# One more set of seven products: the first layer of expert 0 for the last 512 tokens, mixed with second-layer outputs

## The chip, the cores and the metric

The kernel runs on one core of a Trainium2 chip. The metric is device time in microseconds (us). Engine names are those of the profile: PE is the matrix engine, PEld its weight loads, DVE the vector engine, ACT the scalar engine, POOL the GpSimd engine, SP the engine that issues most transfers.

## The reference

Two stages. The first is an attention with positive features: for each of 8 batches and 8 heads, `phi(x) = [exp(p), exp(-p)]` with `p = x @ w_phi` less its largest absolute value; then `phi(q) @ (phi(k)^T v)` divided by `phi(q) . sum(phi(k))`. Its result is the token matrix `x` of 4608 rows and 512 columns. The second is a mixture of 8 experts without selection:

```python
P = np.exp(logits)                      # 4608 x 8, logits = x @ w_gate
for _ in range(8):
    P /= P.sum(1, keepdims=True) + 1e-09
    P /= P.sum(0, keepdims=True) + 1e-09
    P *= N / E
for e in range(E):
    h = np.maximum(x @ w1[e], 0.0)      # 512 -> 1024
    ye = h @ w2[e]                      # 1024 -> 512
    out += P[:, e:e + 1] * ye
```

Every expert works on every token; the eight rounds of row and column scaling are called the routing below.

## The kernel before, in words

**Tokens.** The 4608 tokens lie transposed in the tile `xT`, in nine groups of 512. Groups 0 to 7 hold the first 512 rows of each batch, group 8 the 64 remaining rows of all eight. An accumulator tile `acc[g]` holds the output of a group.

**Expert 0** is computed plainly. `up0(g, part)` (L798) makes two slices of 128 hidden columns of group g: for each, four matmuls of 512 columns into a PSUM bank, then a ReLU on ACT into a tile of the ring `hT` (L776). A group has eight slices. `down0(g, part)` (L802) makes 128 tokens of output: eight matmuls of 512 columns, then a copy into `acc` (L811 on ACT; L818 on DVE for the even parts of groups 0 to 4). Names used below: u60 is part 0 of `up0` for group 6, d53 is part 3 of `down0` for group 5.

**Experts 1 to 7** use seven products instead of eight block products in both layers. `sums_w` (L1014) forms sums and differences of weight quadrants on DVE, some into tiles of the ring `T` (eight tiles). The sums of `x` quadrants are made once: `pair_sums_x(p)` (L1078) for the pairs of groups (0,1), (2,3), (4,5), (6,7), four DVE operations of 1024 columns each into tiles of the ring `S` (five tiles), and `sums_x(8)` (L1094) for group 8, four of 512 columns. All are written to DRAM (`xd`) by SP and read back by `load_x` before each use. `up7` (L1134) makes the first layer. Per block of hidden columns it has the products x1, x2, x3, x4 (which add up in one PSUM bank, an ACT copy L1189 into the ring `U` being taken after each of the first three, and an ACT ReLU L1198 after the last), w1 and w2 in a second bank, y1 in a third. Three DVE operations (L1193) add a bank and a copy, apply the ReLU and write `hT`. For a pair of groups a product is two matmuls of 512 columns (L1163); for group 8 alone four of 256 columns (L1129). `down7` (L1241) makes the second layer, with DVE sums of hidden values into `S` and seven products X1 to Z2. The string `ORDER` (L1407) interleaves a group's `up7` products with the `down7` products of an earlier group, which a list named `queue` holds.

**What sets the order of the work.** Nothing above issues at once. Each call records an operation in a planner (class `Plan`, L112): an engine, an assumed duration, the keys that it reads and writes, and the tiles that it needs. `schedule` then takes, again and again, the operation that can start first by the planner's own clock; among equal starts it takes the one recorded first. A tile ring or a PSUM bank that is not free delays a start. The resulting order on each engine is fixed in the program. On the chip each engine works through its list in order and waits on semaphores.

**Around the change.** The attention stage ends with a planner operation `swap` (L910) that releases the attention's tiles and writes the key "late"; four more `hT` tiles, the rings `T`, `S`, `U`, and the accumulators of groups 5 to 8 exist only from then on. After it come, in the written order: the routing (L937 to 970, eight rounds on DVE, lines L952 to L966, each with one small fp32 matmul of `cs` with `colw` on PE; the result is `P`); the rest of expert 0, `fill` (L908), which alternates the parts of `up0` for groups 6, 7, 8 with the parts of `down0` for groups 5, 6, 7; and then expert 1, with `load_w`, the sums of x, `sums_w` and `up7`. `sums_w` of expert 1 reads `P`, so its DVE operations come after the routing. The first product x1 of expert 1 reads two of those sums and all four tiles that `load_x` brought for the first pair. The list `queue` starts with an empty entry for the first half of expert 1's first pair and the four parts of `down0(8)` for its second half.

Of the kernel before, what the change touches and what calls it, by code (L numbers as in the profile page):

```python
# [12 lines left out]
ALU = mybir.AluOpType  # L13
# [215 lines left out]
def kernel(  # L229
# [535 lines left out]
    def up(w1, g, hT, fcs, n, r=(), w=()):  # L765

        for f0 in fcs[::n]:
            ph = new(f"P{n}")
            ht = hT[f0 // 2]
            for i in range(n):  # L770
# [8 lines left out]
                [ph], [(ht, f0 + i) for i in range(n)])  # L779

    def down(w2, hT, tss, r=()):
        py = new(f"P{len(tss)}")
        for i, ts in enumerate(tss):
            for fc in range(8):
# [4 lines left out]
                    [(hT[f // 2], f) for f in (range(8) if fc == 0 else (fc,))]  # L789
# [13 lines left out]
    def down0(g, part):  # L803
        tss = (part,)
        py = down(W[0][1], hts[g], tss, akey(g))
# [3 lines left out]
        for i, ts in enumerate(tss):  # L809
            if ts % 2 or g >= NA:  # L810
# [126 lines left out]
    def routing():  # L937
        c_bc = None
        for it in range(8):
# [6 lines left out]
            else:  # L946
# [3 lines left out]
                def u(ub=ub):  # L950
# [63 lines left out]
    def sums_w(e, w1, w2):  # L1014

        eng = pool if e == 0 else dve
# [49 lines left out]

    def xq(g, i, j):

        return lambda: xT[:, 2 * i:2 * i + 2, 512 * g + 256 * j:512 * g + 256 * j + 256]
# [8 lines left out]
    def pair_sums_x(p):  # L1078
# [7 lines left out]
        for n, y, z, r in ((0, b12, b11, ["sums of x"]), (1, b22, x(0), [X[0]]),  # L1086
                           (2, b22, b12, []), (3, b21, x(1), [X[1]])):
            sub(dve, 1024, x(n), y, z, ALU.subtract,
# [5 lines left out]
    def sums_x(g):  # L1094

        X = [new("S") for _ in range(2)]

        def x(n):
            return lambda: X[n // 2]()[:, n % 2 * 2:n % 2 * 2 + 2]

        b11, b12, b21, b22 = xq(g, 0, 1), xq(g, 0, 0), xq(g, 1, 1), xq(g, 1, 0)
        for n, y, z, r in ((0, b12, b11, []), (1, b22, x(0), [0]), (2, b22, b12, []),
                           (3, b21, x(1), [1])):
            sub(dve, 512, x(n), y, z, ALU.subtract,
                xkeys(g) + ["late", "sums of x"] + [(X[i // 2], i % 2) for i in r]
                + ([(X[1], "slot")] if n == 2 else []),
                [(X[n // 2], n % 2)] + ([(X[1], "slot")] if n == 0 else []))
        for i in range(2):
            dma("SP", 1 << 18, 250, lambda i=i: nc.sync.dma_start(
                out=Xd[4][i], in_=X[i]().rearrange("p (k a) b -> p k (a b)", k=2)),  # L1110
                [(X[i], n) for n in range(2)], [("Xd", 4, i)])

# [21 lines left out]
    def up7(A, p, X, H, r0):  # L1134
# [3 lines left out]
        gs = (2 * p, 2 * p + 1) if pair else (8,)  # L1138
        xk = [k for g in gs for k in xkeys(g)]

        def b(n):
            i, j = {"11": (0, 1), "21": (1, 1), "22": (1, 0)}.get(n, (0, 0))
            if n[0] != "t":
                if pair:
                    return lambda k: xT[:, 2 * i + k, 1024 * p + 512 * j:][:, 0:512], []
                return lambda k: xT[:, 2 * i + k, 4096 + 256 * j:][:, 0:256], []
            t = int(n[1]) - 1
            if pair:
                return lambda k: X[t]()[:, k, :], [X[t]]
            return lambda k: X[t // 2]()[:, t % 2, 256 * k:256 * k + 256], [X[t // 2]]  # L1150
# [53 lines left out]
        more += [k for n in ("s2", "s3", "22") for k in A[n][1]] + X + list(r0)  # L1204
# [280 lines left out]
```

## Time and profile before

| | us |
|---|---|
| median of three runs | 1029.73 |
| lowest, highest | 1029.61, 1030.56 |
| the profiled execution, device time | 1032.67 |
| its span in the profile | 1030.9 |
| PE busy in the span | 1013.7 |
| DVE, ACT, POOL busy in the span | 861.9, 710.7, 465.0 |

The profiled execution took 2.94 us more than the median; its span leaves out 1.8 us of it. Times of day in the text ("at 246 us") count from the start of the span. A PE row gives the first start, the time from there to the modelled end of the last matmul, the line, and the number of matmuls; as matmuls overlap, the distance between the starts of two rows is the better measure of what the first one took. Idle time ahead of a row, and what ended it, stands in brackets where it is long enough to be shown.

### The profile page before, as it was taken

The page shows a single profiled execution, that of the slowest core. Times are in us where ns is not written, and L with a number is a line of the kernel's source. Part 1 is how long each engine was busy: PE and PEld are TensorE (multiplying, and loading weights), DVE is VectorE, ACT ScalarE, POOL GpSimd, SP SyncE. Part 2 cuts the span into 40 slices and gives each one's busy share as a digit, 9 for nine tenths or more (in the row PEclk, how much of TensorE's full clock was granted, in tenths as well). Part 3 has the DMA queues.
Part 4 walks back from the last instruction along what each step waited for, and adds up shares of the span by engine and source line. Part 5 has one row for each costly group of instructions (what it writes and reads, how often), then busy time and mean ns, then how long its engine had stood idle before and what let it go on. Part 6 is the DMA issues. An engine that isn't in the chain of part 4 may idle for free.

```text
span 1030.9 us, 21864 instructions
## 1 busy us (share of the span) xinstructions
PE 1013.7 (98%) x7958; PEld 690.5 (67%) x7958; DVE 861.9 (84%) x1852; ACT 710.7 (69%) x1577; POOL 465.0 (45%) x534
## 2 busy tenths in 40 slices
PE   7899999999999999999999999999999999999998
PEld 5656666644566766676667766676667666776665
DVE  7999998987777878888888888898878888888776
ACT  7999999846588866665666666665665666665663
POOL 5876765400244354344434454435443544443443
PEclk9999999999999999999999999999999999999999
DMA  9999996085411233121611161116112341103333
GB/s 243 179 172 143 175 167 96 23 212 156 83 42 42 63 85 81 42 63 41 123 42 42 31 124 48 57 32 118 47 43 62 68 98 42 57 27 83 139 126 125
DMA packets 124316, 93.77 MB, mean 91 GB/s; under 512 B 47456, under 2 KB 115872, under 8 KB 124208
## 3 DMA queue, kind: packets, MB, share of 16 engines
q1 hardware_dynamic: 90448, 68.44, 24.9%
q0 software_dynamic: 33680, 23.90, 16.3%
q8 instruction: 62, 1.02, 0.4%
q14 instruction: 46, 0.38, 0.1%
q10 hardware_dynamic: 80, 0.03, 0.0%
HBM read 94.98 MB, written 14.16 MB: 106 GB/s over the span
## 4 chain that ended last, share of the span: by engine, by line
PE 91%; DVE 4%; DMA 3%; SPq 1%; issue 0%; ACT 0%; POOL 0%; DVEq 0%
PE P L1129 40%; PE P L1163 32%; PE P L484 17%; PE P L683 1%; DMA qkT<-qk 1%; DMA acc<-in_q_dram 1%; DVE acc L1302 1%; DVE m L476 1%; DVE w L1012 1%; DMA v_r<-in_v_dram 1%; PE P L722 1%; DVE hT L1193 0%; SPq L406 0%; DVE xb L703 0%; PE P L688 0%
## 5 line engine op out<-in xcount | busy, mean ns | idle before, releaser
L1316 POOL TENSOR_TENSOR acc<-acc,V 128x512 f32<-128x512 f32 x244 | 313.7, 1297 | 421.4 <-ACT V L1312 418.1
L1189 ACT COPY U<-P 128x512 f32<-128x512 f32 x378 | 215.5, 588 | 133.1 <-PE P L1163 105.2
L1312 ACT ACTIVATE V<-P 128x256 f32<-128x256 f32 x488 | 212.4, 475 | 121.3 <-PE P L1129 117.8
L1193 DVE CUSTOM_DVE_ANT_0 hT<-P,U 128x512 bf16<-128x512 f32 x378 | 252.1, 687 | 42.9 <-ACT U L1189 22.9
L1129 PEld LDWEIGHTS <-S 128*128 128x128 bf16 x1984 | 194.1, 98 | 52.6
L1302 DVE SCALAR_TENSOR_TENSOR acc<-P,acc 128x256 f32<-128x256 f32 x372 | 159.8, 477 | 68.4 <-PE P L1129 65.7
L1163 PE MATMUL P<-xT,w 128*128 128x512 bf16 x728 | 200.7, 379 | 1.1 <-DVE acc L1302 1.1
L1129 PEld LDWEIGHTS <-hT 128*128 128x128 bf16 x1488 | 145.6, 98 | 54.8
L1163 PE MATMUL P<-xT,T 128*128 128x512 bf16 x560 | 160.6, 379 | 0.0
L1129 PE MATMUL P<-w,hT 128*128 128x256 bf16 x992 | 143.1, 273 | 0.0
L1129 PE MATMUL P<-T,S 128*128 128x256 bf16 x1056 | 136.8, 273 | 0.0
L1163 PEld LDWEIGHTS <-w 128*128 128x128 bf16 x896 | 87.6, 98 | 61.7 <-issue 0.8
L1129 PE MATMUL P<-w,S 128*128 128x256 bf16 x928 | 123.5, 273 | 0.0
L1012 DVE TENSOR_TENSOR S<-hT 128x512 bf16<-128x512 bf16 x248 | 105.6, 440 | 21.0 <-PE P L1129 20.0
L1163 PEld LDWEIGHTS <-T 128*128 128x128 bf16 x672 | 65.7, 98 | 58.4 <-issue 2.1
L476 DVE TENSOR_REDUCE m<-P 128x4 f32<-128x512 f32 x128 | 83.5, 677 | 3.9 <-PE P L484 3.0
L609 POOL TENSOR_TENSOR v<-v_m,em 128x512 bf16<-128x512 f32 x64 | 66.9, 1045 | 42.7 <-ACT em L480 39.9
L1198 ACT ACTIVATE hT<-P 128x512 bf16<-128x512 f32 x126 | 74.2, 597 | 12.1 <-PE P L1163 11.9
L484 PE MATMUL P<-w,hT 128*128 128x512 bf16 (+1 forms) x328 | 81.7, 374 | 0.2 <-DVE m L476 0.2
L484 PE MATMUL P<-xT,w 128*128 128x512 bf16 x288 | 74.6, 379 | 0.3 <-ACT q L480 0.3
L480 ACT ACTIVATE k<-P 128x512 bf16<-128x512 f32 x128 | 68.5, 628 | 4.3 <-PE P L484 3.0
L480 ACT ACTIVATE q<-P 128x512 bf16<-128x512 f32 x128 | 69.3, 636 | 1.1 <-PE P L484 0.7
(109 smaller groups left out, 1177.2 us busy)
## 6 DMA issues: line engine op xcount, KB each, us to landing
xT<-xd SPq DMA_DIRECT2D x168, 128.0 KB, 2.2
w<-in_moe_w_dram POOLq DMA_DIRECT2D x14, 1024.0 KB, 9.9
v_m<-in_v_dram SPq DMA_DIRECT2D x14, 512.0 KB, 5.1
out_dram<-acc SPq DMA_DIRECT2D x12, 512.0 KB, 3.1
X<-xd SPq DMA_DIRECT2D x42, 128.0 KB, 2.2
early<-xd SPq DMA_DIRECT2D x42, 128.0 KB, 2.2
xd<-S SPq DMA_DIRECT2D x18, 256.0 KB, 3.3
qk<-in_k_dram POOLq DMA_DIRECT2D x12, 256.0 KB, 6.0
```

The lines of the kernel that those rows point to most:

```text
L476: dve(el, lambda: nc.vector.tensor_reduce(out=dst(), in_=src(), axis=AX.X, op=ALU.max, apply_absolute_value=True), r, w)
L480: act(el, lambda: nc.scalar.activation(out=dst(), in_=src(), func=ACT.Exp, bias=0.0, scale=scale), r, w)
L484: nc.tensor.matmul(out_, lhsT=lhsT, rhs=rhs, start=start, stop=stop)
L1012: lambda: f.tensor_tensor(out=out_(), in0=x(), in1=y(), op=op), r, w, **kw)
L1129: pe(256, lambda i=i, k=k, z=z: nc.tensor.matmul(bank()[:, 256 * i:256 * i + 256], lhsT=lhs(k, i), rhs=rhs(k), start=first and z, stop=k = ...
L1163: pe(512, lambda k=k: nc.tensor.matmul(bank[fp](), lhsT=f()[:, k, 128 * fp:128 * fp + 128], rhs=rhs(k), start=first and k == 0, stop=k == ...
L1189: act(512, lambda: nc.scalar.copy(out=u[fp][n]().rearrange("p a b -> p (a b)"), in_=x[fp]()), [x[fp]], [u[fp][n]])
L1193: dve(500, lambda: nc.vector._custom_dve(ADD_SAT, out=out_(fp, i, j), in0=halves_(bank[fp]()), in1=flat(u[fp][n]()), s0=3.0e38, s1=0.0), [ ...
L1198: act(512, lambda: nc.scalar.activation(out=out_(fp, i, j), in_=halves_(x[fp]()), func=ACT.Relu, bias=0.0, scale=1.0), [x[fp]], [okey(fp, ...
L1302: dve(330, lambda n=n, ts=ts: nc.vector.scalar_tensor_tensor(out=acc[g][:, ts, 256 * j:256 * j + 256], in0=bank()[:, 256 * n:256 * n + 256 ...
L1312: act(390, lambda n=n: nc.scalar.activation(out=u()[:, n, :], in_=bank()[:, 256 * n:256 * n + 256], func=ACT.Copy, bias=0.0, scale=P[:, 4 ...
L1316: pool(670, lambda: nc.gpsimd.tensor_tensor(out=acc[g][:, 2 * i:2 * i + 2, 256 * j:256 * j + 256], in0=acc[g][:, 2 * i:2 * i + 2, 256 * j: ...
```

## The change

- `sums_w1_first()` is new: four DVE operations of 1024 columns that form the sums of expert 0's first weight matrix, into four tiles of `T`. The quadrants themselves stay as they are, since `up0` reads them too.
- `sums_x` now takes its two tiles from `T` instead of `S`, and hands them on. For group 8 they are still written to DRAM.
- The calls of `sums_x(8)` and of the four `pair_sums_x` move in the written order from expert 1, behind `fill`, to the place right behind `routing()` and ahead of the rest of expert 0. (The short description says "ahead of the routing"; the call of `routing()` stands first in the diff.)
- Group 8's first layer of expert 0 goes through `up7` with those sums: per block of 256 hidden columns 28 matmuls of 256 columns, three copies and one ReLU (two slices at once) on ACT and three additions on DVE. There are two such blocks.
- `fill` is replaced by a written list, `FILL`: u60 to d62. Behind it the products of group 8 are interleaved by `ORDER` with d63, d70, d71, d72. The list `queue` now holds d73 for the first half of expert 1's first pair; the four parts of `down0(8)` stay in its second half.
- Keys of `hT` tiles are adapted (`hkeys`, `down`, `up`).

```diff
-    def down(w2, hT, tss, r=()):
+                [ph], [(ht, (f0 + i) % 2) for i in range(n)])
+    def hkeys(g, f):
+        return range(2) if g == 8 else (f % 2,)
+
+    def down(g, w2, hT, tss, r=()):
...
-    def expert0(i):
-        if i < 4 * NG:
-            up0(i // 4, i % 4)
-        down0(i // 4 - 1, i % 4)
-
-    fill = range(4 * NA + 4, 4 * NG)
...
-    routing()
-    grant("X", 4, {id(d): d for key in [("L", g) for g in range(NG)] + ["colw"]
-                   for d in plan.readers[key]}.values())
-    for i in fill:
-        expert0(i)
...
+    def sums_w1_first():
+
+        w1 = W[0][0]
+        S = [new("T") for _ in range(4)]
+        wk = [(w1, n) for n in range(4)]
+
+        def q(i, j):
+            return lambda: w1()[:, 2 * j:2 * j + 2, 512 * i:512 * i + 512]
+
+        def s(n):
+            return lambda: S[n]().rearrange("p (a b) -> p a b", a=2)
+
+        for n, y, z, op, r in ((0, q(0, 0), q(0, 1), ALU.add, []),
+                               (2, q(1, 0), q(0, 0), ALU.subtract, []),
+                               (1, s(0), q(1, 0), ALU.subtract, [S[0]]),
+                               (3, q(1, 1), s(1), ALU.subtract, [S[1]])):
+            sub(dve, 1024, s(n), y, z, op, wk + ["late"] + r, [S[n]])
+        return {"11": (q(1, 0), wk), "12": (q(1, 1), wk), "22": (q(0, 1), wk),
+                "s1": (s(0), [S[0]]), "s2": (s(1), [S[1]]), "s3": (s(2), [S[2]]),
+                "s4": (s(3), [S[3]])}
...
     def sums_x(g):
 
-        X = [new("S") for _ in range(2)]
+        X = [new("T") for _ in range(2)]
...
-    def up7(A, p, X, H, r0):
+    def up7(A, p, X, H, r0, g=8):
...
-    queue = [(0, 8, {}, None, None), (0, 8, {"X1": 0, "X2": 1, "Z1": 2, "Y1": 3}, None, None)]
+    FILL = (
+        "u60 u61 u62 u63 d50 u70 d51 u71 d52 u72 d53 u73 d60 d61 d62").split()
+    MIX = ("63", "70", "71", "72")
+    queue = []
...
+    CHUNK = ("X1", "X2", "Z1", "Y1")
+    routing()
+    grant("X", 4, {id(d): d for key in [("L", g) for g in range(NG)] + ["colw"]
+                   for d in plan.readers[key]}.values())
+    A0 = sums_w1_first()
+    X0 = {8: sums_x(8)}
+    for p in range(4):
+        pair_sums_x(p, dve)
+    for i in FILL:
+        (up0 if i[0] == "u" else down0)(int(i[1]), int(i[2]))
+    for g in (8,):
+        H = [[new("hT") for _ in range(2)] for _ in range(2)]
+        hts[g] = H[0] + H[1]
+        un = up7(A0, 5, X0[g], [H], ["late"], g)
+        mix = iter(MIX)
+        for n in ORDER:
+            if len(n) == 3:
+                un[n[:2], int(n[2])]()
+            elif n in CHUNK:
+                i = next(mix, None)
+                if i:
+                    down0(int(i[0]), int(i[1]))
+    queue += [(0, 7, {"Y1": 3}, None, None),
+              (0, 8, {"X1": 0, "X2": 1, "Z1": 2, "Y1": 3}, None, None)]
+
     for e in range(1, E):
...
         if e == 1:
-            for p in range(4):
-                pair_sums_x(p)
-            sums_x(8)
```

More of the change, by code (lines that the diff above doesn't have):

```diff
@@ L1014, in sums_w @@
     def sums_w(e, w1, w2):
-        eng = pool if e == 0 else dve
+        eng = dve
         def q(w, i, j):
@@ L1203, in up7 @@
         more = [("banks", 0), ("banks", 1)]
-        more += [k for n in ("s2", "s3", "22") for k in A[n][1]] + X + list(r0)
+        more += [k for n in ("s2", "s3", "22") for k in A[n][1]] + list(r0)
+        more += [k for _, key in X for k in key]
         def x1(fp):
```

36 lines of the change are left out of this document (21 added, 15 removed).

## The prediction

> **What bounds the kernel now.** I read the head of the page first, then the table of stretches, the waits of PE, and the timelines of PE and DVE from 200 to 285 us, where the change lies.
>
> ```profile
> PE 1013.7 (98%) x7958; PEld 690.5 (67%) x7958; DVE 861.9 (84%) x1852; ACT 710.7 (69%) x1577; POOL 465.0 (45%) x534
> ```
>
> PE is busy for 98% of the span; the rest has to lie in few places. The table of stretches (PE, PEld, DVE, ACT and POOL busy, granted clock, DMA share, GB/s) finds them:
>
> ```profile
> 200.00:250.00 50.00, 49.99 (x343) 25.76 (x342) 41.72 (x98) 27.29 (x52) 2.65 (x5) 1.00 0.63 169
> 250.00:300.00 50.00, 49.55 (x293) 28.43 (x291) 37.49 (x72) 37.32 (x74) 11.40 (x10) 1.00 0.42 85
> ...
> 1000.00:1031.00 31.00, 26.86 (x196) 18.84 (x193) 18.96 (x38) 11.31 (x26) 12.24 (x10) 0.97 0.36 136
> ```
>
> From 200 to 250 us PE has no idle time, from 250 to 300 us 0.45 us, and the last stretch holds the tail. All that PE waited for between 200 and 1000 us is one row:
>
> ```profile
> PE P L1163 <- DVE acc L1302: 1.1, 5, 0.5
> ```
>
> So in the stage of the change, and in all that follows, time is PE work, end to end. A change there gains what it takes off PE and loses each hole that it makes. The granted clock is 1.00 throughout; nothing here moves it.
>
> The profiled execution took 1032.67 us, 2.94 more than the median of 1029.73. My sum is made as a difference against the profiled execution (its span of 1030.9 plus 1.8 around it) and then put on the median.
>
> **PE work.** Removed: 8 slices x 4 matmuls of 512 columns. Their price is the distance between rows of eight:
>
> ```profile
> 246.83 1.89 PE L484 MATMUL P<-xT,w 128*128 128x512 bf16 x8
> 248.56 1.89 PE L484 MATMUL P<-w,hT 128*128 128x512 bf16 x8
> 250.28 0.59 PE L1163 MATMUL P<-xT,w 128*128 128x512 bf16 x2
> ```
>
> 1.73 us for eight, 216 ns each: 32 x 216 = 6.90 us. Added: 7 products x 2 blocks x 4 matmuls = 56 of 256 columns. The same stage, group 8 through seven products mixed with second-layer products, exists for the later experts; the chain has it as one unbroken piece:
>
> ```profile
> 560.70 12.24 PE P L1129 x112
> ```
>
> 12.24/112 = 109.3 ns: 56 x 109.3 = 6.12 us. PE saves 0.78 us. The chunks of the second layer (d63 to d83) are the same in number and move only in order.
>
> [...]
>
> **ACT and DVE work.** Unit prices:
>
> ```profile
> L1193 DVE CUSTOM_DVE_ANT_0 hT<-P,U 128x512 bf16<-128x512 f32 x378 | 252.1, 687 | 42.9 <-ACT U L1189 22.9 <-PE P L1163 11.0 <-PE P L1129 3.0
> L1189 ACT COPY U<-P 128x512 f32<-128x512 f32 x378 | 215.5, 588 | 133.1 <-PE P L1163 105.2 <-PE P L1129 22.1 <-DVE S L1012 0.3
> ...
> L776 ACT ACTIVATE hT<-P 128x512 bf16<-128x512 f32 x72 | 43.1, 635 | 8.9 <-PE P L484 8.8
> ...
> L1012 DVE TENSOR_TENSOR T<-w 128x1024 bf16<-128x1024 bf16 x28 | 20.2, 722 | 0.1
> ```
>
> These are the DVE addition, the ACT copy, the ACT ReLU of 512 columns and the DVE sum of weights. ACT loses 8 ReLUs (5.1 us) and gets 6 copies and 2 ReLUs (4.8 us): nothing to speak of. Its stage has room:
>
> ```profile
> 209.10:246.30 37.20, 37.19 (x194) 17.64 (x191) 30.19 (x68) 18.03 (x32) 1.47 (x2) 1.00 0.83 223
> ```
>
> ACT is busy for 18.0 of these 37.2 us, which is the cover. DVE is another matter: it gets 4 sums of weights x 0.69 (as T<-w) and 6 additions x 0.69, 6.9 us, in a stage in which it is busy for 30.2 of 37.2 us, 7.0 idle. Nearly all of that idle time is inside the routing, while a round waits for PE's small matmul:
>
> ```profile
> L966 DVE RECIPROCAL c_bc<-P 128x8 f32<-128x8 f32 x8 | 1.7, 208 | 6.1 <-PE P L484 5.4 <-ACT acc L811 0.7
> ```
>
> **What moves without cost.** The sums of x are 20 operations before and after. Their new written place can hardly start them earlier: the first five ran at once, and the sixth waited for a tile of `S` to come free.
>
> ```profile
> 212.23 0.63 DVE L1012 TENSOR_TENSOR S<-xT 128x1024 bf16<-128x1024 bf16 x1
> ...
> 224.82 0.64 DVE L1012 TENSOR_TENSOR S<-xT,S 128x1024 bf16<-128x1024 bf16 x1
> ```
>
> The four sums of group 8 do come earlier, since they now take `T`; they leave the stretch behind 235 us and enter the one at 210 us, a zero sum on DVE. Their two writes to DRAM move ahead of eleven others in SP's list; each waits for its two sums. Who needs them is group 8 of expert 1, some 50 us later, and the tiles read back for the first pair are due only when expert 1 begins: 0. `T` has eight tiles: four for the weight sums, two for x, two left for the routing, which holds about one at a time. The sums of expert 1 find two at once and the others when group 8's products end, before they are due: 0, with the risk kept for the range. PSUM: six banks for the two blocks, one for an output chunk, one for the routing's matmul, eight of eight. A late bank would delay a round by about one ACT copy, 0.6 us; I take 0, because the six are not all held at once. POOL's two weight transfers of expert 1 start at "late" as before; the second matrix of expert 2 can be fetched somewhat earlier, since d80 to d83 end earlier; nobody waits for it: 0.
>
> **When expert 1 can begin.** This decides the sign. Rows at the end of the routing (`P`, then sums of expert 1):
>
> ```profile
> 245.96 0.46 DVE L968 TENSOR_TENSOR P<-T,c_bc 128x288 f32<-128x288 f32 x1
> 246.34 0.68 DVE L1012 TENSOR_TENSOR T<-w 128x1024 bf16<-128x1024 bf16 x1
> 247.06 0.69 DVE L1012 TENSOR_TENSOR w<-w 128x1024 bf16<-128x1024 bf16 x1
> 247.78 0.69 DVE L1012 TENSOR_TENSOR T<-w 128x1024 bf16<-128x1024 bf16 x1
> ```
>
> The second T<-w ends at 248.5 us; with it x1 has its operands, and it started at 250.28, 1.8 us later, when PE was done with `fill`. So today the routing has 1.8 us of slack.
>
> The 6.9 us of new DVE work lie ahead of `P`: the weight sums have to precede group 8's products, and these come on PE before the routing ends. Bounds of the delay: 0.8 us if all of 6.1 us of idle time in the L966 row is used, 6.9 us if none is. I take 4.5, nearer the upper end, because a round that has group 8's sums of x ahead of its answer still waited:
>
> ```profile
> 237.92 0.21 DVE L966 RECIPROCAL c_bc<-P 128x8 f32<-128x8 f32 x1 [1.19 <-PE P L484]
> ```
>
> Those 1.19 us passed with DVE empty: the sums at hand had run out or came between the steps, where they delay the chain. x1's operands are then ready at 253.0 us (249.3 to 255.4).
>
> What PE can do without them: all of `fill` (till 250.28), less 0.78, plus d80 to d83, which before lay inside expert 1's first pair:
>
> ```profile
> L484 PE MATMUL P<-w,hT 128*128 128x512 bf16 x32 | 8.5, 379 | 0.0
> ```
>
> 32 x 0.216 = 6.9 us, so till 256.4 us, 3.4 us after the operands. PE need not stop. But those chunks had a use:
>
> ```profile
> L484 PE MATMUL P<-w,hT 128*128 128x512 bf16 x8 | 2.4, 379 | 0.0
> ```
>
> ```profile
> L484 PE MATMUL P<-w,hT 128*128 128x512 bf16 x8 | 2.2, 379 | 0.0
> ```
>
> These rows group PE's timeline from 253.7 to 258.2 and from 265.9 to 269.1 us. The first eight chunk matmuls stand in the first half of the pair, where the written order puts none: the planner pulled them in where a product waited for a copy or an addition. The other eight stand among the second half's last products, by the written order or for the same reason. Without filler the pair would lose between 8 x 0.216 = 1.7 and 16 x 0.216 = 3.5 us. With 3.4 us of it left, it loses between 0 and 0.1. To this I add the sums of expert 1: five of them (S3 and four of w2, 3.5 us at the rows' price) now run when x1 has begun, and delay its additions; before, the 1.8 us of slack let two or three of these run ahead of x1. I take 0.5 us of holes in all, ends 0 and 3.5.
>
> **What PE loses in the routing today.** Rows around three of the small matmuls (two passes each):
>
> ```profile
> 214.28 0.28 PE L484 MATMUL P<-cs,early 128*128 128x8 f32 x2
> 214.42 1.46 PE L484 MATMUL P<-xT,w 128*128 128x512 bf16 x6
> ...
> 217.61 0.36 PE L484 MATMUL P<-cs,early 128*128 128x8 f32 x2
> 217.82 1.89 PE L484 MATMUL P<-xT,w 128*128 128x512 bf16 x8
> 219.55 1.46 PE L484 MATMUL P<-w,hT 128*128 128x512 bf16 x6
> 220.95 0.36 PE L484 MATMUL P<-cs,early 128*128 128x8 f32 x2
> ```
>
> The first takes 0.14 us of PE's time, with no wait. Between the other two lie 14 matmuls, 3.02 us; the distance is 3.34. In sum:
>
> ```profile
> L484 PE MATMUL P<-w,hT 128*128 128x512 bf16 x96 | 23.4, 379 | 0.0
> L484 PE MATMUL P<-xT,w 128*128 128x512 bf16 x85 | 20.3, 379 | 0.0
> L484 PE MATMUL P<-cs,early 128*128 128x8 f32 x16 | 2.6, 233 | 0.0
> ```
>
> 181 x 0.216 + 8 x 0.14 = 40.2 of the 41.0 us from 209.3 to 250.28: 0.8 us are lost by waiting. With more DVE work between the steps the planner may place these matmuls better or worse: between -0.8 and +0.8, I take 0, the middle, as the rows show both a matmul without a wait and two with one.
>
> **Sum.** -0.78 + 0.5 = -0.3 us: the profiled execution would take 1032.4, the median 1029.4 us. This is within 0.2% (2.06 us), which is about what a measurement of this kernel can tell from no change.
>
> **Rivals.**
>
> 1. Slower: expert 1 waits for the routing. DVE at 81% gets 6.9 us more in the one serial chain of the stage. If x1's operands come late, chunks d80 to d83 are used up ahead of x1, the first pair loses up to 3.5 us, and beyond 256.4 us PE stands still one for one. The loss reaches 2.06 us above before when the holes reach 2.84 us, with operands at 255.7 us: 2.7 us later than I think and just past the upper bound of the DVE sum. For it: the planner puts x1 at the moment at which it believes the sums ready, so the old slack of 1.8 us is gone, and the planner believes rounds shorter than they are (3.02 against 3.34 us). Against: 7.0 us of idle DVE time, and rounds that hold PE and DVE in step. Typical price: operands at 257.5 us, 1.1 idle + 3.5 - 0.78 = +3.8, 1033.5 us.
>
> 2. Faster: DVE work fills the waits of the rounds, PE's 0.8 us there go, and the 0.45 us that PE lacks in the stretch from 250 to 300 us goes with the new order: -0.78 - 0.8 - 0.45 = -2.0, 1027.7 us, just about the bound. Against: all three at once, and the filler stays whole.
>
> 3. A matmul of 256 columns costs more than half of one of 512. By rows 109.3 against 108 ns, 56 x 1.3 ns = 0.07 us, in the sum already. [...]
>
> 4. The change does not do what it says: x sums are not earlier. That is what I expect of all but group 8's, at no price.
>
> **Chances.** My forecast 0.54; the first rival 0.36, since its deciding point lies 0.3 us past my bound for the delay, while the lost slack can add to it, and all unlisted mishaps of a re-planned order (a bank, a `T` tile) end in the same wait; the second 0.09, being the sum of all gains that the trace offers; the third 0.01, ending within 0.2%. The likeliest case alone reaches from -1.5 (1028.2) to +2.0 (1031.7). The range goes from 1028.2, which leaves out most of the second rival, to 1033.5, which takes in over half of the first: 2 in 10 remain outside.
>
> **What would show it.** PE's matmuls of 256 columns at L1129's successor grow by 56, those of 512 columns fall by 32. The last `P` operation of the routing at 249 to 252 us instead of 246; the first L1163 product of expert 1 between 252 and 255 us, with d80 to d83 partly ahead of it. No idle time of PE before 255 us. If rival 1 holds, the waits of PE show a product waiting for DVE (a sum of w, or L1193) by some us between 250 and 275. From there on the trace should be the old one, shifted. Wrong would be made: sums of expert 1 waiting for `T`, weight sums of expert 0 so late that group 8's products hold up PE, or a later stage that the new order disturbs.

## The result, and the profile after

| | before | after |
|---|---|---|
| median of 20 runs each, us | 1030.48 | 1028.55 |
| the profiled execution, device time, us | 1032.67 | 1028.92 |
| its span, us | 1030.9 | 1027.1 |

The ratio is 0.9982, 95% interval 0.9975 to 0.9989: 1.9 us faster (1.1 to 2.6). That is within 0.2%, but on its edge and six times the 0.3 us of the forecast. One of the 20 runs of the kernel after took 1305.84 us at a granted clock of 0.76; it is left out of the ratio, and the median is the same without it. The question is where the other 1.6 us came from.

First the head of the page of the kernel after, its table of stretches from 200 to 300 us (PE, PEld, DVE, ACT, POOL busy, granted clock, DMA share, GB/s), and all that PE waited for between 200 and 1000 us:

```profile
span 1027.1 us, 21923 instructions
...
PE 1011.5 (98%) x7982; PEld 692.4 (67%) x7982; DVE 867.6 (84%) x1862; ACT 710.4 (69%) x1577; POOL 465.7 (45%) x534
```

```profile
200.00:250.00 50.00, 50.00 (x354) 28.03 (x351) 44.68 (x104) 26.24 (x48) 2.46 (x3) 1.00 0.73 180
250.00:300.00 50.00, 50.00 (x307) 29.91 (x306) 40.56 (x80) 38.27 (x77) 13.96 (x11) 1.00 0.34 74
```

```profile
PE P L1181 <- DVE acc L1321: 0.6, 4, 0.2
```

PE has 24 more matmuls (56 less 32), DVE 10 more operations. DVE went from 41.7 to 44.7 us busy in the stretch up to 250 us, and PE has no idle time in either stretch; the 0.45 us that it lacked behind 250 us before is gone.

A difference of two spans mixes two things. The row of 32 gate matmuls is the last before the stage that differs, and the first product of expert 1 for group 8 alone is the first after it. Both rows from PE's timeline, before and then after (start, time, engine, line, operation, tiles, count):

```profile
208.51 0.94 PE L484 MATMUL P<-wgate,xT 128*128 128x8 bf16 x32
...
343.00 0.60 PE L1129 MATMUL P<-xT,w 128*128 128x256 bf16 x4
```

```profile
206.49 0.94 PE L484 MATMUL P<-wgate,xT 128*128 128x8 bf16 x32
...
339.21 0.60 PE L1144 MATMUL P<-xT,w 128*128 128x256 bf16 x4
```

From row to row 134.49 us before and 132.72 after: 1.77 less. From the second row to the end of the span it is 687.9 us in both (1030.9 - 343.00, 1027.1 - 339.21). The other 2.0 us of the difference of spans lie ahead of the gate row, where PE's order is the same in both kernels. In the second profile of the kernel after (below) the gate row stands at 205.52, in other kernels of this study between 205.7 and 208.5: it moves between executions. So the distance from the gate row to the second row, called the stage distance below, tells more than a span. Its -1.77 us agrees with the -1.9 us of the medians.

Now the routing. From the timelines of DVE (the first and last of group 8's four sums of x, then the end of the routing) and of PE in the kernel after:

```profile
210.20 0.36 DVE L1002 TENSOR_TENSOR T<-xT 128x512 bf16<-128x512 bf16 x1
...
212.09 0.42 DVE L1002 TENSOR_TENSOR T<-xT,T 128x512 bf16<-128x512 bf16 x1
...
246.79 0.46 DVE L964 TENSOR_TENSOR P<-T,c_bc 128x288 f32<-128x288 f32 x1
247.17 0.68 DVE L1002 TENSOR_TENSOR T<-w 128x1024 bf16<-128x1024 bf16 x1
247.88 0.69 DVE L1002 TENSOR_TENSOR w<-w 128x1024 bf16<-128x1024 bf16 x1
248.61 0.69 DVE L1002 TENSOR_TENSOR T<-w 128x1024 bf16<-128x1024 bf16 x1
```

```profile
241.24 0.36 PE L484 MATMUL P<-cs,early 128*128 128x8 f32 x2
...
246.37 3.83 PE L484 MATMUL P<-w,hT 128*128 128x512 bf16 x17
250.03 0.81 PE L1181 MATMUL P<-xT,w 128*128 128x512 bf16 x3
```

`P` comes 40.30 us after the gate row (246.79 - 206.49), before 37.45: the routing is 2.85 us later. x1 of expert 1 starts 0.7 us after the end of its second sum (249.30), where there had been 1.8 us. Seventeen chunk matmuls in a row lead up to it without a gap; 18 were left for the first pair, 32 before.

### The profile page after: what moved, and what is told of

The parts are those of the page before. It is cut to its first block, busy times and chain, and to the rows that moved or that the text cites. A ratio compares the mean times of both kernels' runs of the same rounds, so it can differ in the third digit from the quotient of the medians.

```text
span 1027.1 us, 21923 instructions
## 1 busy us (share of the span) xinstructions
PE 1011.5 (98%) x7982; PEld 692.4 (67%) x7982; DVE 867.6 (84%) x1862; ACT 710.4 (69%) x1577; POOL 465.7 (45%) x534
## 4 chain that ended last, share of the span: by engine, by line
PE 93%; DVE 4%; ACT 2%; issue 1%; DMA 0%; DVEq 0%; POOLq 0%
PE P L1144 41%; PE P L1181 32%; PE P L484 18%; PE P L683 1%; DVE acc L1321 1%; DVE w L1002 1%; ACT q L480 1%; ACT k L480 1%; DVE m L476 1%; PE P L722 1%; DMA wphi_f<-in_w_phi_dram 0%; DVE hT L1211 0%; DVE xb L703 0%; PE P L688 0%; DVE P L695 0%
## 5 line engine op out<-in xcount | busy, mean ns | idle before, releaser
L1207 ACT COPY U<-P 128x512 f32<-128x512 f32 x384 | 219.5, 587 | 133.3 <-PE P L1181 105.1
L1211 DVE CUSTOM_DVE_ANT_0 hT<-P,U 128x512 bf16<-128x512 f32 x384 | 256.5, 687 | 36.3 <-ACT U L1207 20.8
L1181 PE MATMUL P<-xT,w 128*128 128x512 bf16 x728 | 200.8, 379 | 0.6 <-DVE acc L1321 0.6
L484 PE MATMUL P<-xT,w 128*128 128x512 bf16 x256 | 66.7, 379 | 0.3 <-ACT q L480 0.3
```

The lines of the kernel that those rows point to most:

```text
L484: nc.tensor.matmul(out_, lhsT=lhsT, rhs=rhs, start=start, stop=stop)
L1181: pe(512, lambda k=k: nc.tensor.matmul(bank[fp](), lhsT=f()[:, k, 128 * fp:128 * fp + 128], rhs=rhs(k), start=first and k == 0, stop=k == ...
L1207: act(512, lambda: nc.scalar.copy(out=u[fp][n]().rearrange("p a b -> p (a b)"), in_=x[fp]()), [x[fp]], [u[fp][n]])
L1211: dve(500, lambda: nc.vector._custom_dve(ADD_SAT, out=out_(fp, i, j), in0=halves_(bank[fp]()), in1=flat(u[fp][n]()), s0=3.0e38, s1=0.0), [ ...
```

## The experiments

All distances in this table count from the gate row of the same profile. "x1" is expert 1's first product, "chunks" the second-layer matmuls of expert 0 that PE runs after it, "stage distance" the distance to expert 1's first product for group 8.

| kernel | `P` | x1 | chunks | stage distance | ratio to before, 95% |
|---|---|---|---|---|---|
| before | 37.45 | 41.77 | 32 | 134.49 | |
| after | 40.30 | 43.54 | 18 | 132.72 | 0.9982, 0.9975 to 0.9989 |
| after_again | 40.30 | 43.55 | 18 | 132.73 | 0.9982, 0.9973 to 0.9991 |
| e1_plain8 | 35.67 | 39.78 | 40 | 133.61 | 0.9991, 0.9982 to 1.0000 |
| e2_sums_moved | 37.44 | 41.76 | 32 | 134.49 | 1.0001, 0.9992 to 1.0011 |
| e5_fill | 37.37 | 40.61 | 37 | 134.57 | 1.0008, 0.9998 to 1.0017 |
| e9_T8first | 35.69 | 41.52 | 32 | 133.74 | 0.9996, 0.9986 to 1.0005 |
| e3_dve4 | 42.76 | 46.00 | 6 | 133.58 | 0.9991, 0.9982 to 1.0000 |
| e3_dve10 | 46.68 | 48.63 | 0 | 137.90 | 1.0032, 1.0020 to 1.0044 |
| e4_groups78 | 42.69 | 47.27 | 32 | 140.49 | 1.0061, 1.0048 to 1.0074 |
| e8_78spread | 45.14 | 48.38 | 21 | 138.44 | 1.0038, 1.0023 to 1.0053 |
| e6_pool | 69.19 | 71.98 | 0 | 161.04 | 1.0261, 1.0246 to 1.0276 |
| e8b_78spreadpool | 69.84 | 71.14 | 0 | 160.43 | 1.0271, 1.0254 to 1.0288 |

The stage distance repeats to 0.01 us in the two profiles of the kernel after, while the ratio's interval is about 1 us to either side. Small effects are therefore read from the distance. Its differences to before agree with the ratios wherever these are large enough to tell: e4 +6.0 us against 0.61% (6.3 us), e8 +3.95 against 0.38% (3.9).

### The kernel after once more

No edit.

> The changed kernel once more, to see what of the 3.8 us between the two profiled spans belongs to the change. Up to the 32 gate matmuls the order of PE is the same in both kernels, and yet that row starts at 208.51 us before and at 206.49 us after. My theory: these 2.0 us are chance (arrival of the first inputs), and the change itself is 1.16 us in the stage (from that row to the first second-layer product of expert 1: 60.94 us before, 59.78 after) and 0.6 us behind it (761.45 against 760.83 us). Expected: gate row anywhere between 206 and 209 us, stage 59.8 +-0.1, rest 760.8 +-0.3, time 1.8 us below before. Rival: the start itself is faster with the new program; then the gate row stands near 206.5 us again and time is some 3 us below before.

The same ratio, and the stage distance the same to 0.01 us, though the gate row moved from 206.49 to 205.52, lower than expected. To the first second-layer product it is 59.79 us, behind it 760.8 us, both as expected.

### Without the seven products

The kernel after, with its order, its sums of x and its `T` tiles, but group 8's first layer of expert 0 plain:

```diff
-    A0 = sums_w1_first()
-    X0 = {8: sums_x(8)}
+    sums_x(8)
...
-    for g in (8,):
-        H = [[new("hT") for _ in range(2)] for _ in range(2)]
...
+    for i in "u80 d63 u81 d70 u82 d71 u83 d72".split():
+        (up0 if i[0] == "u" else down0)(int(i[1]), int(i[2]))
```

> The changed kernel without the seven products: group 8 of expert 0 plain, u80 to u83, alternating with d63, d70, d71, d72; no sums of expert 0's weights; x sums at their new written place, FILL and d73 in expert 1's first pair as in the changed kernel. Theory A (the gain is PE work, 0.78 us, plus smaller waits in the routing that come with more work beside it): stage 60.6 us, between 60.3 and 61.0, time 0.3 to 1.5 us below before. Theory B (the new order alone gives the gain, the seven products nothing): stage 59.8 us as in the changed kernel, time 1.8 us below before.

From the table: 133.61. So the seven products are worth 133.61 - 132.72 = 0.89 us, near the 0.78 us of PE work worked out beforehand. The remaining 0.1 us is not assigned to single rows. But one half of the gain (134.49 - 133.61 = 0.88 us) is there without them. The first theory had the numbers (60.67 us to the first second-layer product, some 0.9 us below before by the ratio), but not where this half comes from. The next three runs look for it.

### Only the place of the sums of x

The kernel before, with its own `S` tiles and its own `fill`, all sums of x moved in the written order:

```diff
-    routing()
-    grant("X", 4, {id(d): d for key in [("L", g) for g in range(NG)] + ["colw"]
-                   for d in plan.readers[key]}.values())
-    for i in fill:
-        expert0(i)
...
+    routing()
+    grant("X", 4, {id(d): d for key in [("L", g) for g in range(NG)] + ["colw"]
+                   for d in plan.readers[key]}.values())
+    for p in range(4):
+        pair_sums_x(p)
+    sums_x(8)
+    for i in fill:
+        expert0(i)
...
-            for p in range(4):
-                pair_sums_x(p)
-            sums_x(8)
```

> The kernel before with one thing of the change: the sums of x (pairs, then group 8, in tiles of S as before) written right behind the routing instead of behind fill. The measure here is M, from the gate row to the first product of group 8 in expert 1: 134.49 us before, 132.73 in the changed kernel, 133.61 in the one with group 8 plain. That last one has 0.88 us of gain without seven products. Theory A (it comes from FILL and from d73 standing in expert 1's first pair): M 134.5 +-0.1, time as before. Theory B (it comes from the place of the sums of x): M 133.6, time 0.9 us below before.

Nothing: 134.49 as before, and `P` at the same place to 0.01 us. The planner had them there already.

### Only the written list and d73

The kernel before with the order of the written list, group 8 plain in it, and d73 in the first half of expert 1's first pair:

```diff
-    for i in fill:
-        expert0(i)
+    FILL = (
+        "u60 u61 u62 u63 d50 u70 d51 u71 d52 u72 d53 u73 d60 d61 d62 "
+        "u80 d63 u81 d70 u82 d71 u83 d72").split()
+    for i in FILL:
+        (up0 if i[0] == "u" else down0)(int(i[1]), int(i[2]))
...
-    queue = [(0, 8, {}, None, None), (0, 8, {"X1": 0, "X2": 1, "Z1": 2, "Y1": 3}, None, None)]
+    queue = [(0, 7, {"Y1": 3}, None, None), (0, 8, {"X1": 0, "X2": 1, "Z1": 2, "Y1": 3}, None, None)]
```

> The kernel before with the other thing: the written list u60 to d62 and then u80 d63 u81 d70 u82 d71 u83 d72, and d73 in the first half of expert 1's first pair; the sums of x at their old place and in S. Theory A: M 133.6 +-0.1, time 0.9 us below before. Theory B: M 134.5, time as before. If it takes both, something between.

134.57, 0.08 more than before. Neither of the two alone is the missing 0.88 us. One difference between e1 and before is in neither of these runs: group 8's sums stand first and lie in `T` tiles.

### Group 8's sums of x in `T` and first, all else as before

The kernel after with before's `fill` and queue, and group 8 plain:

```diff
-    A0 = sums_w1_first()
-    X0 = {8: sums_x(8)}
+    sums_x(8)
...
-    for i in FILL:
-        (up0 if i[0] == "u" else down0)(int(i[1]), int(i[2]))
...
+    for i in range(4 * NA + 4, 4 * NG):
+        up0(i // 4, i % 4)
+        down0(i // 4 - 1, i % 4)
...
-    queue += [(0, 7, {"Y1": 3}, None, None),
+    queue += [(0, 8, {}, None, None),
```

> The kernel before, with a third thing that the changed kernel has: right behind the routing the four sums of group 8 come first and go into tiles of T, then those of the pairs; fill and the empty entry of expert 1's first half as before. Neither the place alone (in S, group 8 last: M 134.49) nor the list FILL with d73 alone (134.57) gave the 0.88 us that the changed kernel with group 8 plain has (133.61). There the end of the routing, the operation that writes P, is at 35.67 us after the gate row; in the other three at 37.4. Theory A (the early sums of group 8 end the routing 1.8 us sooner, and this is the whole cause): P at 35.7, M 133.6, time 0.9 us below before. Theory B (an earlier P is worth something only if d73 then fills expert 1's first pair): P at 35.7, but M 134.3 to 134.6, time as before.

Found: 133.74, 0.75 us less than before. (The ratio, 0.9986 to 1.0005, cannot tell this from nothing.) `P` is 1.76 us sooner (35.69). These are nearly the numbers of the first theory, but not its cause. In the kernel before, PE's timeline has one idle gap between the gate row and expert 1's group 8, in front of the second half of the second pair. PE's rows there, before and then in e9:

```profile
281.94 1.04 PE L1129 MATMUL P<-w,hT 128*128 128x256 bf16 x8
283.42 1.89 PE L1163 MATMUL P<-xT,w 128*128 128x512 bf16 x8 [0.45 <-DVE acc L1302]
```

```profile
281.46 1.04 PE L1144 MATMUL P<-w,hT 128*128 128x256 bf16 x8
282.33 1.89 PE L1181 MATMUL P<-xT,w 128*128 128x512 bf16 x8
```

In e2 and e5 the same gap is there (0.46 and 0.45 us); in e9, e1 and after it is gone. By the profile the product waited for an addition of the second layer (L1302), which empties a PSUM bank. From start to start it costs more than its 0.45 us: 1.48 us before, 0.87 in e9, so 0.61. From the gate row to expert 1's first second-layer product e9 has 60.80 us, before 60.94: 0.14 us. The two make up the 0.75 us.

This split tells more when it is made for more runs. Behind the first second-layer product the stage distance has 73.55 or 73.56 us left in before, e2, e5 and e4 (below), and 72.94 us in e9, e1, after and e8 (below): with the stop and without. Ahead of it stand 60.94 us before, 60.93 in e2, 61.02 in e5, 60.80 in e9, 60.67 in e1 and 59.78 in after.

So the stop is not tied to an early `P`: after has `P` later than before and no stop. Nor do early sums in `T` suffice to be rid of it: e4 has them, and the stop too (0.46 us at 287.04). PE and DVE work in the same order in both kernels there, yet in e9 the product starts at 282.33, ahead of the end of the first of the four additions that begin at 282.03 (about 0.47 us each); so it waits for none of them. Another PSUM bank, chosen by the planner in the new order, would do that; the rows do not show the bank. Whether `T` or the first place of the sums brought about this order was not told apart, since the edit has both.

The differences from run to run are: before to e9 -0.75, e9 to e1 (list and d73, now on top of the early sums) -0.13, e1 to after (seven products) -0.89, together -1.77, as they must be. Split the other way, the stop is worth 0.61 us, and the order ahead of the first second-layer product 0.14 + 0.13 = 0.27 us.

### More work for DVE in the same stage

The kernel after with 4 or 10 more DVE operations of 1024 columns behind the four sums of group 8 and ahead of those of the pairs. They write a tile that nobody reads.

```diff
+    D0 = new("V")
+    for n in range(4):
+        sub(dve, 1024, lambda: bf(D0).rearrange("p a b -> p (a b)").rearrange("p (a b) -> p a b", a=2), lambda: W[0][0]()[:, 0:2, 0:512],
+            lambda: W[0][0]()[:, 2:4, 0:512], ALU.add, [(W[0][0], i) for i in range(4)] + ["late"], [D0])
```

> The changed kernel with four more DVE operations of 1024 columns behind group 8's sums of x (2.7 us), to find from where a late routing costs. With ten of them M rose from 132.73 to 137.90 us, since all of d73 and d80 to d83 were used up ahead of expert 1 and its first pair had holes. Theory A (free as long as filler is left): operands at 42.8 + 2.7 = 45.5 us after the gate row, 3.0 us of other PE work left: M 132.7 to 133.3, time still 1.2 to 1.8 us below before. Theory B (in proportion to the DVE work, 4/10 of 5.2 us): M 134.8, time as before or above.

> The changed kernel with ten more DVE operations of 1024 columns written behind the sums of x of group 8, whose result nobody reads: 10 x 0.68 = 6.8 us of DVE work ahead of the end of the routing, nothing else changed. This prices a late routing. In the changed kernel the operands of expert 1 are ready 42.8 us after the gate row, and PE has other work till 48.5. Price of the prediction's rival 1: operands up to 49.6, 1.1 us past that, plus 1.7 to 3.5 us for the lost filler: stage 62.6 to 64.4 us, time 1 to 3 us above before. If filler does not matter: stage 59.8 to 61. If DVE's idle time takes half of it: operands at 46.2, stage 59.8 to 61 as well, and PE without idle time.

This asks how near the kernel is to the first rival of the prediction. With four (2.7 us of DVE) `P` is 2.46 us later than in after and the stage distance 0.86 us longer, between the two theories of its expectation and nearer to the first. PE has one gap, right behind the pair's products:

```profile
267.88 1.59 PE L1144 MATMUL P<-w,hT 128*128 128x256 bf16 x13 [0.62 <-DVE hT L1211]
```

With ten (6.8 us) `P` is 6.4 us later and the stage distance 5.18 us longer. All chunks are used up ahead of x1, and the pair has gaps:

```profile
248.47 0.36 PE L484 MATMUL P<-cs,early 128*128 128x8 f32 x2 [1.18 <-DVE cs L957]
248.68 3.18 PE L484 MATMUL P<-w,hT 128*128 128x512 bf16 x14
...
255.76 0.59 PE L1181 MATMUL P<-xT,w 128*128 128x512 bf16 x2 [0.84 <-ACT acc L814]
...
258.68 0.59 PE L1181 MATMUL P<-xT,T 128*128 128x512 bf16 x2 [1.46 <-ACT U L1207]
...
262.53 0.38 PE L1181 MATMUL P<-xT,T 128*128 128x512 bf16 x1 [0.25 <-DVE hT L1211]
...
271.85 1.59 PE L1144 MATMUL P<-w,hT 128*128 128x256 bf16 x13 [0.32 <-DVE hT L1211]
```

The gap at 248.47 is PE standing still for the routing; the four from 255.76 on (2.87 us) are the pair without its filler, the last of them right behind its products; they lie inside the 1.7 to 3.5 us that the prediction gave for that loss. (The five gaps are 4.05 of the 5.18 us; the rest is not assigned. To the first second-layer product it is 62.01 us, a little less than the 62.6 to 64.4 expected.) The first rival's mechanism exists. The kernel after has between 0 and 2.7 us of DVE work left until it begins.

### Two groups by seven products

The kernel after with group 7 treated like group 8. (Not shown: the keys of `hT` for group 7, and its sums of x, which go into the two tiles of `V`.)

```diff
-        "u60 u61 u62 u63 d50 u70 d51 u71 d52 u72 d53 u73 d60 d61 d62").split()
-    MIX = ("63", "70", "71", "72")
+        "u60 u61 u62 u63 d50 d51 d52 d53").split()
+    MIX = {7: ("60", "61", "62", "63"), 8: ("70", "71", "72")}
...
-    X0 = {8: sums_x(8)}
+    X0 = {7: sums_x(7), 8: sums_x(8)}
...
-    for g in (8,):
+    for g in (7, 8):
```

> The changed kernel with group 7 of expert 0 through seven products too (its x sums in the two tiles of V, which lie idle then; FILL ends with d53; group 7 mixed with d60 to d63, group 8 with d70 to d72). PE loses another 0.78 us; DVE gets 4 sums of 512 columns (1.4 us) and 6 additions (4.1 us) more ahead of the routing's end. Theory A (DVE work costs nothing while PE has other work): operands of expert 1 at 42.8 + 5.5 = 48.3 us after the gate row at the latest, PE's other work till 48.5 - 0.8 = 47.7: stage between 59.0 and 61, likeliest 59.3; time 2 to 2.6 us below before. Rival 1 of the prediction (PE waits for the routing and expert 1's first pair loses its filler): stage 61 to 63 us, time equal to before or 1 us above.

Not a second 0.89 us but 7.8 us lost against after, more than either theory had. PE starves in the middle of group 7. Its timeline, and the table of stretches over the place (granted clock in the third column from the right):

```profile
230.19 0.60 PE L1147 MATMUL P<-V,w 128*128 128x256 bf16 x4
...
233.99 0.41 PE L484 MATMUL P<-cs,early 128*128 128x8 f32 x2 [3.20 <-DVE cs L957]
235.88 1.01 PE L1147 MATMUL P<-V,w 128*128 128x256 bf16 x4 [1.47 <-ACT U L1210]
...
238.39 1.06 PE L1147 MATMUL P<-xT,w 128*128 128x256 bf16 x4
239.24 1.06 PE L1147 MATMUL P<-T 128*128 128x256 bf16 x4
240.09 1.06 PE L1147 MATMUL P<-xT,w 128*128 128x256 bf16 x4
```

```profile
230.60:236.00 5.40, 0.73 (x5) 0.46 (x4) 5.40 (x12) 1.46 (x3) 0.00 (x0) 0.83 0.86 293
236.00:241.00 5.00, 5.00 (x25) 3.43 (x24) 3.65 (x8) 1.18 (x2) 0.00 (x0) 0.50 0.48 153
241.00:245.00 4.00, 4.00 (x23) 2.10 (x22) 3.29 (x7) 1.07 (x2) 0.00 (x0) 1.00 0.00 0
```

DVE is busy without a break (5.40 of the 5.40 us) while PE waits for it. Then PE pays a second time: after the two gaps the granted clock is 0.50 from 236 to 241 us, rows of four matmuls of 256 columns stand 0.85 us apart (238.39, 239.24, 240.09) instead of 0.44 (223.98 to 224.42 in the same timeline), and some 2.5 us more are gone (an estimate, half of the 5 us). If the clock fell from 1.00 to 0.50 in one step, a mean of 0.83 over the 5.40 us puts the fall at about 234.2 us, 3.4 us after PE ran out of work at 230.8 (an estimate), with 3.20 of these us idle.

Was it the want of second-layer chunks beside group 7? The next kernel keeps more chunks for later: d50 to d53 beside group 7, d60 to d63 beside group 8, and d70 to d73 beside the first half of expert 1's first pair:

```diff
-        "u60 u61 u62 u63 d50 d51 d52 d53").split()
-    MIX = {7: ("60", "61", "62", "63"), 8: ("70", "71", "72")}
+        "u60 u61 u62 u63").split()
+    MIX = {7: ("50", "51", "52", "53"), 8: ("60", "61", "62", "63")}
...
-    queue += [(0, 7, {"Y1": 3}, None, None),
+    queue += [(0, 7, {"X1": 0, "X2": 1, "Z1": 2, "Y1": 3}, None, None),
```

> Groups 7 and 8 through seven products as in the kernel that took 6 us more, with the output chunks spread otherwise: only u60 to u63 written ahead of group 7, d50 to d53 mixed into group 7, d60 to d63 into group 8, d70 to d73 into the first half of expert 1's first pair and d80 to d83 into the second. In that kernel PE had nothing else to do in the midst of group 7 and waited 3.2 and 1.5 us for the routing and a copy, after which its clock was at 0.50 for some 5 us. Theory A (want of filler): no wait above 1 us, clock 1.00 throughout, M between 132 and 135.5 us (132.73 - 0.78, plus up to 3.5 for filler missing in expert 1's first pair). Theory B (DVE's extra 5.5 us as such): a wait for the routing of over 2 us again, M above 137.

Better by 2.05 us than e4, still 5.7 us behind after. The written spreading did not survive the planner: it ran 27 chunk matmuls in one piece, and a gap of 4.20 us follows soon after, this time for an addition of group 7 on DVE.

```profile
224.96 5.99 PE L484 MATMUL P<-w,hT 128*128 128x512 bf16 x27
...
235.93 1.01 PE L1147 MATMUL P<-xT,T 128*128 128x256 bf16 x4 [4.20 <-DVE hT L1214]
```

From 236 to 241 us the granted clock is 0.50 here too. (In the same way a mean of 0.82 from 230.9 to 236 us puts the fall 2.4 us after PE ran out of work, an estimate; so the two traces give no sharp length.) By its numbers (a wait above 2 us, 138.44) this looks like the second theory, but the kernel did not test what it was meant to test: chunks beside group 7 at the moment of the gap were in neither run. What stands is that PE lacks work exactly while DVE has the routing, the sums of x and group 7's additions at once. Which part is want of filler and which is DVE stays open.

### Sums of the pairs on POOL

The kernel after, and the one with two groups, with the sixteen sums of the pairs moved from DVE to POOL:

```diff
-        pair_sums_x(p, dve)
+        pair_sums_x(p, pool)
```

> The changed kernel with the sums of x of the four pairs on POOL instead of DVE (16 operations of 1024 columns). POOL does almost nothing between 209 and 250 us, DVE is at 89%. Theory A (DVE work is not what bounds the changed kernel, PE has no holes): P 4 to 7 us earlier, at 33 to 36 us after the gate row, and M still 132.4 to 132.8. Theory B (the routing's waits on PE shrink further): M 132.3 or less. Rival: POOL and DVE hold each other up, since POOL's operation on SBUF tiles of 512 fp32 columns takes 1.3 us; should one of 1024 columns take 2.6 us, the last comes 42 us after the gate row, the tiles that hold x sums for expert 1's first pair are read back late, and M rises by 2 us or more.

> Groups 7 and 8 through seven products with the spread output chunks (M 138.44 us, PE stood 4.2 us for an addition of group 7 on DVE, then ran at half clock), and the pairs' sums of x on POOL. If DVE's work is what broke that kernel, 9.6 us less of it mend it: no wait above 1 us, M between 131.8 and 132.6 (132.73 less 0.78, plus little), time 2 to 3 us below the kernel before, better than the changed one. If the want of other PE work in the midst of group 7 broke it, a wait of 2 us or more stays, M above 134.

This was to give DVE its time back. Instead both kernels lose 2.6 to 2.7%: the rival of the first expectation, which had 2 us or more, came with 28 us against after. DVE's and POOL's timelines of e6:

```profile
208.49 0.36 DVE L953 RECIPROCAL rr<-rr 128x36 f32<-128x36 f32 x1
208.78 9.79 DVE L1002 TENSOR_TENSOR T<-w 128x1024 bf16<-128x1024 bf16 x1
218.49 2.37 DVE L954 TENSOR_TENSOR T<-early,rr 128x288 f32<-128x288 f32 x1
...
223.30 0.66 DVE L957 TENSOR_REDUCE cs<-T 128x8 f32<-128x288 f32 x1
```

```profile
209.67 2.14 POOL L1002 TENSOR_TENSOR S<-xT,S 128x1024 bf16<-128x1024 bf16 x1
211.76 2.12 POOL L1002 TENSOR_TENSOR S<-xT 128x1024 bf16<-128x1024 bf16 x1
213.83 2.11 POOL L1002 TENSOR_TENSOR S<-xT,S 128x1024 bf16<-128x1024 bf16 x1
215.90 2.11 POOL L1002 TENSOR_TENSOR S<-xT 128x1024 bf16<-128x1024 bf16 x1
218.09 2.45 POOL L1002 TENSOR_TENSOR S<-xT,S 128x1024 bf16<-128x1024 bf16 x1
```

A DVE sum that takes 0.69 us alone takes 9.79 us: it ends 0.6 us after four POOL operations, back to back, have ended. (When it began, at 208.78, POOL was issuing a weight transfer; its spans are rough.) The next one, 0.45 us elsewhere, takes 2.37 us and ends 0.3 us after the fifth. DVE's reductions, with one input, keep their times beside POOL's sums (0.66 us at 223.30, 0.67 in after). The routing then holds PE up twice for long. PE's timeline; for the first gap the profile names a transfer of the sums as the last to finish, while what the small matmul reads is DVE's reduction `cs`, which ends at 223.96:

```profile
224.16 0.56 PE L484 MATMUL P<-cs,early 128*128 128x8 f32 x2 [12.30 <-DMA xd<-S]
...
267.28 0.56 PE L484 MATMUL P<-cs,early 128*128 128x8 f32 x2 [5.74 <-DVE cs L957]
```

In this trace the DVE operations that take several times as long beside POOL's sums have two inputs. The first DVE sum lasted over four POOL operations, the next over one. What made them wait, and why the first got no turn in between, is not shown.

PE's seven gaps in e6 between the gate row and expert 1's group 8 come to 22.0 us, most of the 28.3 us lost against after; behind the first long one the granted clock has a mean of 0.83 from 225 to 240 us, behind the second of 0.78 from 268 to 275 us, which makes about 6 and 4 us at 0.50 (an estimate, if it was either 0.50 or 1.00). e8b has the same stop of 12.30 us, so it does not tell its two theories apart.

No kernel of this study was faster than after.

## Why the prediction was right, and where it was wrong

- **PE saves 0.78 us by the seven products: right.** Measured 0.89 us (e1 to after). The price of 256 columns at half of 512 holds: in the kernel after, rows of four of them stand 0.44 us apart (236.88 to 237.32), rows of eight of 512 columns 1.73 us (234.72 to 236.45), 109 against 216 ns for one.
- **The four sums of group 8 "leave the stretch behind 235 us and enter the one at 210 us, a zero sum on DVE": the step that failed.** The move itself was seen rightly, the price was not: 0.75 us (before to e9). Counted as busy time it is a zero sum: from 0.5 us behind the start of the gate row to `P` DVE is busy for 29.9 us before and 30.1 in e9, and all twenty sums stand ahead of `P` in both. But `P` came 1.76 us sooner, because more of the sums fell into the waits of the rounds: DVE's idle time there fell from 6.1 us (the row of L966 in the prediction) to 4.1 in e9:

```profile
L962 DVE RECIPROCAL c_bc<-P 128x8 f32<-128x8 f32 x8 | 1.7, 208 | 4.1 <-PE P L484 3.9 <-ACT acc L814 0.2
```

Of these 1.76 us PE gained 0.14. The other 0.61 us are the stop at 283 us, which the order that the planner then made does not have. That part could not have been read from the profile of before; it is luck of the new order, since e4, with early sums in `T`, has the stop again.

- **The other sums of x at no price: right** (e2, 0.00).
- **DVE's 6.9 us delay `P` by 4.5 us (0.8 to 6.9): mechanism right, size too large.** Against before the delay is 2.85 us. Against e1, which has the early sums but not the new DVE work, it is 40.30 - 35.67 = 4.63 us. The 4.5 us were about right for the part that they described; the earlier `P` of the failed step (1.76 us in e9) was missing from it.
- **PE need not stop before expert 1: right.** x1 stands at 250.03 with no idle time ahead of it.
- **Holes of 0.5 us in expert 1's first pair: wrong, 0.** With `P` earlier than thought, 18 of 32 chunk matmuls were left as filler; the prediction had 16 left (3.4 us) and still charged 0.5 us for late sums of expert 1. The gap of before at 283 us, which the prediction left standing, went.
- **PE's waits in the routing unchanged: roughly right.** Of eight small matmuls four had the longer row (0.36 us) before, two after (241.24 is one). At 0.2 us each that would be some 0.4 us; e9 and e1 still have three such rows. What the runs show ahead of the first second-layer product, apart from the seven products, is 0.27 us, not assigned to single rows.
- **First rival (expert 1 waits for the routing): not reached, but real.** e3_dve10 shows all of it, +5.18 us for 6.8 us of DVE work.
- **Second rival (-2.0 us): nearest in size, and in part in its terms.** It had 0.78 us of PE work (0.89 measured), the gap at 0.45 (0.61 from start to start) and the waits in the routing at 0.8 (at most 0.27). Its cause, new DVE work that fills the waits of the rounds, was not needed: e9 has none, there the sums of x fill 2.0 us of the waits, and that brought PE 0.14 us.

As a difference the time came out between the forecast (-0.3 us) and the second rival (-2.0 us), at -1.77, just outside the likeliest case's own range of -1.5 to +2.0. As a time, 1028.55 us lies just above the lower end of 1028.2 only because before, too, was 0.75 us slower in this measurement than in the three runs on which the forecast stands (1030.48 against 1029.73); that is luck. The forecast of a change within 0.2% held because what was missed is small, not because the sum was complete: 0.5 us of holes did not come, the stop of 0.61 us went, 0.27 us went ahead of the first second-layer product, and the seven products brought 0.11 us more. These are the 1.49 us between -0.28 and -1.77.

## What to carry to other kernels

Moving work within an engine's list can be a zero sum in busy time and still change how long a dependent chain waits: here `P` came 1.76 us sooner with the same DVE work ahead of it. How much of that reaches the engine that bounds the kernel is another question, here 0.14 us. And an order that is planned anew can lose or gain a stop far from what was changed (0.61 us here), so a forecast to a few tenths of a microsecond needs a range for that. To attribute a microsecond in a kernel of a thousand, measure between two marker rows that both kernels share; here that distance repeated to 0.01 us in two profiles of one kernel, where the runs spread by over 1 us. An engine with a few microseconds of slack on paper may have much less: 2.7 us more on DVE cost 0.86 us, 6.8 us cost 5.18.

## What the runs showed of the hardware that was not expected

- Two gaps of PE, 3.20 and 1.47 us, were followed by about 5 us at a granted clock of 0.50 (e4), a single one of 4.20 us likewise (e8; both from 236 to 241 us). Each of these stops cost some 2.5 us beyond its own length (an estimate, half of the 5 us). Gaps of 0.25 to 1.46 us in e3_dve10 left the clock at 1.00.
- Beside a stream of POOL operations that read SBUF a DVE operation with two SBUF inputs lasted over four of them: 9.79 us instead of 0.69 (e6). Later ones lasted over one (2.37 us instead of 0.45) or three (6.63 us at 259.81, also instead of 0.45).
- The time from the start to the gate row differs by up to 3 us between the profiled executions (205.52 to 208.53 us), by 0.97 between two of one kernel, with the same work of PE ahead of it.
